# Summary scores of both query halves in 64-column halves of the array, and two groups of an expert's first step planned among the last blocks of the expert before

## The chip, the cores and the metric

The kernel runs on one NeuronCore of a Trainium2 chip. The metric is the device time of one execution in microseconds (us). Before the change four runs gave 669.8, 669.79, 671.92 and 669.19 us; their median is 669.8 us.

The core has five engines that run their own instruction streams and wait for each other through semaphores: TensorE (PE in the profile; its weight loads, which run beside the matmuls, are PEld), VectorE (DVE), ScalarE (ACT), GpSimd (POOL) and SyncE (SP). In this kernel POOL and SP mostly issue transfers.

## The reference

The first part is an attention over 4 batches, 8 heads, 768 positions and 64 numbers per head. Each query sees the keys within 15 positions of its own, and beside them 24 summaries, each standing for a block of 32 keys. The result goes into a mixture of 8 experts in which every token goes through every expert, weighted by a matrix that is normalised by rows and by columns in eight rounds.

```
k_sum = k.reshape(B, H, nb, 32, D).max(axis=3)
v_sum = v.reshape(B, H, nb, 32, D).mean(axis=3)
scores_l = scale * q @ k.T, kept where |i - j| < 16
scores_s = scale * q @ k_sum.T + log(32)
a = softmax(concat(scores_l, scores_s));  attn = a @ concat(v, v_sum)

x = attn as (3072, 512);  P = exp(x @ w_gate - max)
8 times: P /= rowsum(P); P /= colsum(P); P *= N / E
out = sum over e of P[:, e] * (relu(x @ w1[e]) @ w2[e])      # w1: 512x1024, w2: 1024x512
```

## The kernel before, in words

**Attention.** Two heads make a pair; 16 pairs, 0 to 15, four to a batch. Pairs 0 to 3 (the first batch) are worked in query halves (`pair_half`), pairs 4 to 15 whole (`pair_whole`). For a whole pair the steps on the engines are these:

- `tr` (L300) transposes keys and queries on PE for pairs 4 to 11; for pairs 12 to 15 `tr_dma` (L327) does it with a DMA that SP issues.
- `key_max` (L332, DVE) reduces the transposed keys `kT` to 24 block maxima `ks`; `key_max_split` (L338, DVE) writes them into `ksT`, columns 0 to 31 for the first head and 32 to 63 for the second, other rows zeroed. Columns 64 to 127 of `ksT` are zero.
- `scores` (L344, PE) makes the windowed scores: contraction over 64 rows, the two heads in the two row halves of the array. `score_exp` (L403, ACT) takes their exponential; `masks` (L407) and `edges` (L415, L419) on DVE cut the window out.
- `summaries` (L449, PE) multiplies all 128 columns of `ksT` with one half of the queries, 384 columns, into a PSUM bank `ss`. It is called once for each of the two query halves, each with a bank of its own. `summary_exp` (L459, ACT) reads the first 64 partitions of each.
- `near_values` (L372, L374) moves the values of neighbouring blocks into `Ve` by four small DMAs, for pairs below 12 from SP, for the others from POOL. `block_sums` (L352, PE) sums values by block.
- `values` (L430, L436, PE) makes the weighted values `av` of one half of the pair, `normalize` (L527, L528, DVE) divides, `to_xT` (L535, PE) or a DMA (L545) transposes into `xT`.

**Expert 0** needs no wait for the whole batch of tokens: when half a batch of `xT` is there (eight halves of 384 tokens), `expert0` runs its hidden layer (L208, 8 groups of 4 matmuls of 384 columns) and its projection (L213, matmuls of 512 columns), whose unscaled result is copied into `out_acc` (L204). These matmuls fill PE while the attention's vector work runs.

**Routing.** After the last batch's logits (`logits`, L555) the eight rounds of normalisation start. Each takes four DVE instructions (`sink_rows`, L564 to L568), a small matmul (`sink_cols`, L574) and two more DVE instructions (`sink_apply`, L577, L578). The last round gives `P`.

**Experts 1 to 7** use seven products for each two by two block product. Tokens are taken in three groups of 1024 for each expert (`g` counts the groups through all experts). The first step of a group consists of four `quad`s: seven products of two matmuls of 512 columns each (L742), with copies (L204), sums and relus (L764, L199) between them, and sums of the hidden blocks (`h_sum`, L776). The second step of a group consists of four `pair`s (L793), whose results are scaled by `P` and added into `out_acc`. Sums of tokens (`x_sum`, L696) and of weights (`w1_sum`, L707; `w2_sum`, L717) come before. The weights of expert 1 are loaded by POOL after the last transposed `xT` has landed.

**Order.** Nothing in the text of the kernel fixes the order on an engine. A small planner (`Plan`) holds every step as a unit with an engine, an assumed cost, its dependencies, a priority (the lower comes first) and the PSUM buffers that it opens. It simulates the engines with these costs, and where several units could start within 0.02 us of each other on an engine, it takes the one with the lowest priority number. The instructions are then issued in the planned order, and every engine runs its own list strictly in that order. So a changed cost, dependency or priority can move instructions on every engine. PSUM banks are rings in the plan: three `m` banks (expert 0, among others), three `a` banks (attention, among others), one double bank `s` for scores. The units that the change touches, and those around them:

```
U["ss", i, h] = add("PE", 0.17, lambda h=h: summaries(i, h, "a"),
                    [U["km", i], U["kT", i, 1], U.get(("A", i - NE, 1))], prio, opens=[buf])
U["sx", i, h] = add("ACT", 0.46, lambda h=h: summary_exp(i, h), [U["ss", i, h]], prio, uses=[buf])
pr = 1000.0 + n                              # expert 0's half n, 0 to 7
pr = 2000.0 + 10.0 * (HF * g + q)            # quad q of group g
```

Of the kernel before, what the change touches and what calls it, by code (L numbers as in the profile page):

```python
# [33 lines left out]
class Plan:  # L34
# [7 lines left out]
    def add(self, eng, cost, fn, deps=(), prio=0.0, opens=(), uses=(), lag=0.0):  # L42
        u = Unit(eng, cost, fn, [d for d in deps if d is not None], prio, list(opens), lag)
        for b in list(opens) + list(uses):
            b.users.append(u)
        if uses and eng != "PE":
            u.prio -= 100.0
        self.units.append(u)
        return u
# [79 lines left out]
def kernel(  # L129
# [10 lines left out]
    nc = tc.nc  # L140
# [12 lines left out]
    W = 16  # L153
    LIVE = 128 + 2 * W
    PADL = LIVE + 2 * W
    HS = S // 2
# [61 lines left out]
    NB = PB  # L218
    NE = 2
# [3 lines left out]
    with tc.manual_schedule():  # L223
# [11 lines left out]
        qT = [attn.tile([128, W + S + W], BF16, name=f"qT{i}") for i in range(NB)]  # L235
        kT = [attn.tile([128, S], BF16, name=f"kT{i}") for i in range(NB)]
# [13 lines left out]
        HF = KF // 2  # L250
# [8 lines left out]
        def bank(tag, name, dtype=FP32):  # L259
            pool, n = (mps, 3) if tag == "m" else (aps, NA)  # L260
            return pool.tile([128, 2048 // mybir.dt.size(dtype)], dtype, tag=tag, name=name, bufs=n)
# [177 lines left out]
        def summaries(i, h, tag):  # L439
            r = i % NB  # L440
            ss, rhs = bank(tag, "ss"), qT[r][:, W + h * HS:W + (h + 1) * HS]
            at["ss", i, h] = ss
            if i < PB and not h:
                for j in range(2):
                    p = slice(64 * j, 64 * j + 64)
                    nc.tensor.matmul(ss[32 * j:32 * j + 32, 0:HS], lhsT=ks[r][p, 0, :], rhs=rhs[p],
                                     start=True, stop=True)
                return
            nc.tensor.matmul(ss[:, 0:HS], lhsT=ksT[r][:], rhs=rhs, start=True, stop=True)  # L449

        def summary_exp(i, h):
            if i < PB:
# [469 lines left out]
        def pair_whole(i, prio):  # L922
            U["near", i] = add("SP" if i < BY_DMA else "POOL", 2.4 if i < BY_DMA else 3.0, lambda: near_values(i),
                               [U["v", i], U.get(("A", i - NE, 1)), U["vc", i % NE]], prio, lag=3.5)
            x1 = []
            deps = [U["kT", i, 0], U["kT", i, 1], U.get(("ed", i - 2))]
            bufs = [Buffer("s")] + (2 * [None] if i < WHOLE else [Buffer("a"), Buffer("a")])
            U["S", i, 0] = U["S", i, 1] = add("PE", 0.4 if i < WHOLE else 0.6, lambda: scores(i), deps, prio,
                                              opens=[x for x in bufs if x is not None])
            U["X", i, 0] = add("ACT", 0.97, lambda: score_exp(i, 0), [U["S", i, 0]], prio, uses=bufs[:1])  # L930
            if i < WHOLE:
                buf = Buffer("s")
                U["S", i, 1] = add("PE", 0.4, lambda: scores_1(i), deps, prio, opens=[buf])
                U["X", i, 1] = add("ACT", 0.97, lambda: score_exp(i, 1), [U["S", i, 1], U["X", i, 0]], prio,
                                   uses=[buf])
            else:
                x1 = [add("ACT", 0.53, lambda j=j: score_exp(i, 1, j), [U["S", i, 0], U["X", i, 0]], prio,
                          uses=bufs[1 + j:2 + j]) for j in range(2)]
                U["X", i, 1] = x1[1]
            for h in range(2):  # L940
                U["mk", i, h] = add("DVE", 0.56, lambda h=h: masks(i, h),
                                    [U["X", i, h], *x1[:h], U.get(("A", i - 2, 1))], prio)
            U["ed", i] = add("DVE", 0.78, lambda: edges(i),
                             [U["X", i, 0], U["X", i, 1], U["mk", i, 1], U.get(("A", i - NE, 1)), U["ec", i % NE]], prio)
            for h in range(2):
                buf = Buffer("a")
                U["ss", i, h] = add("PE", 0.17, lambda h=h: summaries(i, h, "a"),
                                    [U["km", i], U["kT", i, 1], U.get(("A", i - NE, 1))], prio, opens=[buf])
                U["sx", i, h] = add("ACT", 0.46, lambda h=h: summary_exp(i, h), [U["ss", i, h]], prio, uses=[buf])
            for h in range(2):  # L950
                buf = Buffer("a")
                U["A", i, h] = add("PE", 0.4, lambda h=h: values(i, h),
                                   [U["mk", i, h], U["ed", i], U["sx", i, h], U["Vs", i], U["near", i]],
                                   prio, opens=[buf])
                U["no", i, h] = add("DVE", 0.75, lambda h=h: normalize(i, h),
                                    [U["A", i, h], U.get(("x", i - 2))], prio, uses=[buf])
            if i >= X_BY_DMA and i % PB < PB - 1:
                U["xt", i] = add("SP", 1.5, lambda: x_dma(i), [U["no", i, 0], U["no", i, 1]], prio)
                U["x", i] = add("DMA", 1.7, None, [U["xt", i]], prio, lag=2.0)
                return  # L960
            buf = Buffer("a")
            U["xt", i] = add("PE", 0.35, lambda: to_xT(i), [U["no", i, 0], U["no", i, 1]], prio, opens=[buf])
            U["x", i] = add({"ACT": 0.8, "DVE": 0.55}, 0, lambda: x_out(U["x", i].on, i), [U["xt", i]], prio,
                            uses=[buf])
# [156 lines left out]

        def quad(e, p, q):
            g = (e - 1) * NPAIR + p
            pr = 2000.0 + 10.0 * (HF * g + q)
            buf = {t: Buffer(t) for t in "ARQ"}
            old = [U["Yp", (g - 2) // NPAIR + 1, (g - 2) % NPAIR, c, n] for c in range(4) for n in range(1, 8)] if g >= 2 else (
                [] if 2 * g + q // 2 != 3 else [U["pj", h0, c] for h0 in halves[-2:] for c in range(HG)])

            def mul(n, deps, opens=False):
                tag = {2: "R", 5: "Q", 3: "Q"}.get(n, "A")  # L1130
                u = add("PE", 0.435, lambda: product(e, p, q, n), deps, pr,
                        **{"opens" if opens else "uses": [buf[tag]]})
                U["C", e, p, q, n] = u
                return u

            def keep(n, dep):
                u = add(ANY, 0, None, [dep], pr, uses=[buf["Q" if n == 5 else "A"]])
                u.fn = lambda: snap(u.on, e, p, q, n)
                return u

            def fin(blk, deps):
                return add("DVE", 0.7, lambda: add_relu(e, p, q, blk), deps + old, pr,
                           uses=[buf[("R", "Q", None, "A")[blk]]])

            def evac(blk, dep):
                u = add("ACT", 0.6, None, [dep] + old, pr, uses=[buf["AR"[blk == 0]]])
                u.fn = lambda: evac_relu(u.on, e, p, q, blk)
                return u

            W, X = (lambda i: U["w1", e, i]), (lambda i: U["x", p, i])  # L1150
            p1 = mul(1, [U["w1", e]], True)
            sd = add(ANY, 0, None, [p1, U["bits"]], pr - 100.0, opens=[buf["R"]])
            sd.fn = lambda: seed(sd.on, e, p, q)
            buf["A"].users.append(sd)
            p2 = mul(2, [sd])
            c11 = evac(0, p2)
            p5 = mul(5, [W(0), X(0)], True)
            s5 = keep(5, p5)
            p6 = mul(6, [sd, W(1), X(1)])
            s6 = keep(6, p6)  # L1160
            p7 = mul(7, [s6, W(3), X(3)])
            c22 = fin(3, [p7, s5])
            p3 = mul(3, [s5, W(2)])
            c12 = fin(1, [p3, s6])
            p4 = mul(4, [c22, X(2)])
            c21 = evac(2, p4)
            U["H", e, p, q] = [c11, c12, c21, c22]
            if q % 2:
                h = U["H", e, p, q - 1] + U["H", e, p, q]
                d1 = add("DVE", 0.69, lambda: h_sum(e, p, q // 2, 0), h, pr - 90.0)  # L1170
                d2 = add("DVE", 0.69, lambda: h_sum(e, p, q // 2, 1), [d1], pr - 90.0)
                d3 = add("DVE", 0.69, lambda: h_sum(e, p, q // 2, 2), [d2], pr - 90.0)
                d4 = add("DVE", 0.69, lambda: h_sum(e, p, q // 2, 3), [d1], pr - 90.0)
                U["D", e, p, q // 2] = {1: h, 2: h, 4: h, 5: [d1], 6: [d2], 3: [d3], 7: [d4]}
# [120 lines left out]
```

## Time and profile before

| what | value |
|---|---|
| median of four runs | 669.8 us |
| the profiled execution, its own time | 669.8 us |
| its span, first to last instruction | 667.8 us |
| granted TensorE clock | 1.0 in nearly all of the span |
| PE busy | 658.6 us, 99% |
| DVE busy | 548.0 us, 82% |
| ACT busy | 410.2 us, 61% |
| POOL busy | 198.2 us, 30% |
| chain that ended last | PE 94%, DVE 3%, DMA 2% |
| attention and expert 0 | up to about 119 us |
| routing rounds beside the rest of expert 0 | 119 to 147 us |
| experts 1 to 7 | 150 us to the end |

The profile comes from one execution, which took 2.0 us more than its span. A matmul's row gives its start and its modelled length, which is longer than the distance to the next matmul's start, since matmuls follow each other through the array. So "busy" on PE hides short waits: what PE really loses is found from the distances between starts.

### The profile page before, as it was taken

To read this page: it belongs to the slowest core of one execution; us is meant where nothing else is said; L and a number is where in the kernel's file an instruction comes from. 1 tells how busy PE (TensorE), PEld (TensorE's weight loads), DVE (VectorE), ACT (ScalarE), POOL (GpSimd) and SP (SyncE) were. 2 spreads that over 40 slices of the span, in tenths; PEclk is the share of its full clock that TensorE was granted. 3 is DMA by queue.
4 is the path that set the end of the run, shared out by engine and by line. 5 is a ranking of instruction groups with operands and counts; after the bars stand their busy time and mean duration, and the time that the engine had idled before them with its cause. 6 is when DMAs were issued, how large, how long until landed. Compare 5 with 4: busy or idle time off the path is not lost.

```text
span 667.8 us, 13271 instructions
## 1 busy us (share of the span) xinstructions
PE 658.6 (99%) x5131; PEld 436.1 (65%) x5131; DVE 548.0 (82%) x1034; ACT 410.2 (61%) x769; POOL 198.2 (30%) x256
## 2 busy tenths in 40 slices
PE   8999999999999999999999999999999999999996
PEld 4666656654666666666666666666666666666665
DVE  7889968799879787888789887888778877988776
ACT  6667765559855656566555665656565656556652
POOL 8899713000222121222221222222122213222123
PEclk9999999999999999999999999999999999999999
DMA  9999962707333747473654756473847465334656
GB/s 167 176 146 143 130 84 43 127 1 126 56 56 65 127 67 124 75 130 65 95 98 74 125 83 106 70 126 61 123 71 128 79 95 95 64 64 111 158 134 198
DMA packets 112542, 67.89 MB, mean 102 GB/s; under 512 B 77920, under 2 KB 90464, under 8 KB 112480
## 3 DMA queue, kind: packets, MB, share of 16 engines
q0 software_dynamic: 94800, 57.46, 65.0%
q1 hardware_dynamic: 17152, 9.58, 6.1%
q8 instruction: 40, 0.66, 0.4%
q14 instruction: 22, 0.18, 0.1%
q10 hardware_dynamic: 528, 0.02, 0.0%
HBM read 52.45 MB, written 6.29 MB: 88 GB/s over the span
## 4 chain that ended last, share of the span: by engine, by line
PE 94%; DVE 3%; DMA 2%; issue 0%; ACT 0%; SPq 0%; DVEq 0%
PE yps L793 22%; PE pA L742 22%; PE pY L793 17%; PE pQ L742 11%; PE hps L208 5%; PE pR L742 5%; PE yps L213 5%; DMA kT<-kst 1%; PE sg L344 1%; PE av L497 1%; DMA kvf<-in_v_dram 1%; PE vs L352 1%; PE ss L449 1%; PE tx L535 1%; PE tkq L300 1%; PE av L436 1%
## 5 line engine op out<-in xcount | busy, mean ns | idle before, releaser
L793 PEld LDWEIGHTS <-h 128*128 128x128 f16 x2352 | 230.1, 98 | 90.2 <-issue 1.0
L821 POOL DMA_DIRECT2D out_acc<-y x120 | 101.3, 879 | 388.1 <-ACT y L817 107.3
L817 ACT ACTIVATE y<-pY,P_sb 128x256 f32<-128x256 f32 x168 | 79.9, 476 | 130.1 <-PE pY L793 128.2
L808 DVE SCALAR_TENSOR_TENSOR out_acc<-yps,P_sb,out_acc 128x512 f32<-128x512 f32 x128 | 95.1, 745 | 29.1 <-PE yps L793 29.0
L776 DVE TENSOR_TENSOR h<-h 128x1024 f16<-128x1024 f16 x168 | 109.0, 684 | 1.4
L793 PE MATMUL pY<-w,h 128*128 128x256 f16 x672 | 100.3, 273 | 0.6 <-ACT y L817 0.6
L742 PE MATMUL pA<-xT,w 128*128 128x512 f16 x336 | 98.4, 379 | 0.4 <-DVE snap L204 0.4
L793 PE MATMUL yps<-w2sum,h 128*128 128x256 f16 x672 | 98.2, 273 | 0.0
L793 PE MATMUL yps<-w,h 128*128 128x256 f16 x672 | 93.8, 273 | 0.0
L808 DVE SCALAR_TENSOR_TENSOR out_acc<-pY,P_sb,out_acc 128x512 f32<-128x512 f32 x84 | 62.9, 749 | 32.5 <-PE pY L793 31.2
L742 PEld LDWEIGHTS <-w 128*128 128x128 f16 x672 | 65.7, 98 | 32.4 <-issue 1.2
L742 PEld LDWEIGHTS <-w1sum 128*128 128x128 f16 x504 | 49.3, 98 | 45.0 <-issue 0.5
L764 DVE CUSTOM_DVE_ANT_0 h<-pQ,snap 128x512 f16<-128x512 f32 x84 | 57.6, 685 | 5.8 <-ACT snap L204 3.6
L764 DVE CUSTOM_DVE_ANT_0 h<-pA,snap 128x512 f16<-128x512 f32 x84 | 57.4, 683 | 5.7 <-PE pA L742 5.4
L199 ACT ACTIVATE h<-pA 128x512 f16<-128x512 f32 x84 | 50.7, 603 | 11.4 <-PE pA L742 11.2
L199 ACT ACTIVATE h<-pR 128x512 f16<-128x512 f32 x84 | 50.1, 596 | 7.0 <-PE pR L742 6.8
L793 PE MATMUL pY<-w2sum,h 128*128 128x256 f16 x336 | 50.4, 273 | 0.0
L204 ACT COPY pR<-pA 128x512 f32<-128x512 f32 x81 | 46.3, 571 | 6.2 <-PE pA L742 5.4
L742 PE MATMUL pA<-xsum,w 128*128 128x512 f16 x168 | 50.0, 379 | 0.0
L742 PE MATMUL pQ<-xT,w1sum 128*128 128x512 f16 x168 | 50.0, 379 | 0.0
L742 PE MATMUL pA<-xsum,w1sum 128*128 128x512 f16 x168 | 50.0, 379 | 0.0
L742 PE MATMUL pQ<-xsum,w1sum 128*128 128x512 f16 x168 | 50.0, 379 | 0.0
(145 smaller groups left out, 851.7 us busy)
## 6 DMA issues: line engine op xcount, KB each, us to landing
out_acc<-y POOLq DMA_DIRECT2D x120, 256.0 KB, 3.3
w<-in_moe_w_dram POOLq DMA_DIRECT2D x15, 1024.0 KB, 9.6
out_dram<-out_acc SPq DMA_DIRECT2D x24, 256.0 KB, 2.5
qst<-in_q_dram POOLq DMA_DIRECT2D x32, 96.0 KB, 5.6
vx<-in_v_dram POOLq DMA_DIRECT2D x15, 192.0 KB, 6.7
kst<-in_k_dram POOLq DMA_DIRECT2D x24, 96.0 KB, 6.0
w<-in_moe_w_dram POOLq DMA_DIRECT2D x4, 256.0 KB, 7.0
kst<-in_k_dram POOLq DMA_DIRECT2D x3, 192.0 KB, 4.4
```

The source lines that it names most:

```text
L199: nc.scalar.activation(out=out, in_=in_, func=AF.Relu, bias=0.0, scale=1.0)
L204: (nc.scalar.copy if eng == "ACT" else nc.vector.tensor_copy)(out=out, in_=in_)
L208: nc.tensor.matmul(hp[:, 0:n], lhsT=w1s[e][:, dk, f * 128:(f + 1) * 128], rhs=xT[:, dk, t0:t0 + n], start=(dk == 0), stop=(dk == KD - 1))
L213: nc.tensor.matmul(yp[:, d], lhsT=h[:, f, c * 128:(c + 1) * 128], rhs=w2s[e][:, f, d], start=(f == 0), stop=(f == KF - 1))
L300: nc.tensor.transpose(t[:, g * 128:(g + 1) * 128], st[:, g, :, :].rearrange("p j d -> p (j d)"), ident)
L742: nc.tensor.matmul(dst[:], lhsT=lhsT, rhs=rhs, start=first and k == 0, stop=k == HK - 1, skip_group_check=True)
L764: nc.vector._custom_dve(dve_ops.TENSOR_ADD_SAT, out=ring(e, p, q)[:, q % 2, blk, :], in0=at[src, e, p, q][:], in1=at.pop(("snap", n, e, p, ...
L776: nc.vector.tensor_tensor(out=h[:, :, out_, :], in0=h[:, :, a, :], in1=h[:, :, b, :], op=op)
L793: nc.tensor.matmul(dst[:, d], lhsT=lhsT, rhs=rhs, start=f == 0 and n in (1, 5, 2), stop=f == HF - 1, skip_group_check=True)
L808: nc.vector.scalar_tensor_tensor(out=o, in0=y, scalar=scalar, in1=o, op0=ALU.mult, op1=ALU.add)
L817: nc.scalar.activation(out=at[key][:, d], in_=src, func=AF.Copy, bias=0.0, scale=P_sb[:, t, e:e + 1])
L821: nc.gpsimd.dma_start(out=o, in_=at.pop(("y", e, p, c, key))[:], accum_op=ALU.add)
```

## The change

Two edits.

1. For the whole pairs (4 to 15) the two calls of `summaries` become one unit, `summaries_2`. It uses only the 64 columns of `ksT` that are not zero, and issues two matmuls of 384 columns: the first half of the queries goes into partitions 0 to 63 of a PSUM bank, the second half into partitions 64 to 127 of the same bank. The planner's cost is 0.22 for both instead of 0.17 for each, and one `a` bank is opened instead of two. `summary_exp` reads its 64 partitions as before.
2. The priority of the quads of groups 0 and 1 (expert 1's first 2048 tokens) is no longer 2000 and more, but between 1006 and 1007.75, and so among those of expert 0's last two halves (1006 and 1007).

```
+        def summaries_2(i):
+            r, ss = i % NB, bank("a", "ss")
+            for h in range(2):
+                at["ss", i, h] = ss[64 * h:64 * h + 64]
+                nc.tensor.matmul(ss[64 * h:64 * h + 64, 0:HS], lhsT=ksT[r][:, 0:64],
+                                 rhs=qT[r][:, W + h * HS:W + (h + 1) * HS], start=True, stop=True)
...
+            buf = Buffer("a")
+            U["ss", i, 0] = U["ss", i, 1] = add("PE", 0.22, lambda: summaries_2(i),
+                                                [U["km", i], U["kT", i, 1], U.get(("A", i - NE, 1))], prio, opens=[buf])
             for h in range(2):
-                buf = Buffer("a")
-                U["ss", i, h] = add("PE", 0.17, lambda h=h: summaries(i, h, "a"),
-                                    [U["km", i], U["kT", i, 1], U.get(("A", i - NE, 1))], prio, opens=[buf])
                 U["sx", i, h] = add("ACT", 0.46, lambda h=h: summary_exp(i, h), [U["ss", i, h]], prio, uses=[buf])
...
         def quad(e, p, q):
             g = (e - 1) * NPAIR + p
-            pr = 2000.0 + 10.0 * (HF * g + q)
+            pr = 2000.0 + 10.0 * (HF * g + q) if g > 1 else 1006.0 + 0.25 * (HF * g + q)
```

## The prediction

> **What bounds the kernel now.** I read the engine lines of the page first, then the groups by line, then PE's timeline by starts, the chain, and DVE's share by windows.
>
> ```profile
> PE 658.6 (99%) x5131; PEld 436.1 (65%) x5131; DVE 548.0 (82%) x1034; ACT 410.2 (61%) x769; POOL 198.2 (30%) x256
> ...
> L449 PE MATMUL ss<-qT,ksT 128*128 128x384 bf16 x28 | 8.6, 329 | 0.0
> ...
> L446 PE MATMUL ss<-qT,ks 64*32 64x384 bf16 x8 | 1.3, 332 | 0.0
> ```
>
> PE sets the time. Taking for each shape the distance between starts where matmuls follow each other (0.216 us for 512 columns, 0.109 for 256, 0.162 for 384), all PE distances that are longer than that add up to 17 us of the span; from 180 to 640 us they add up to nothing. So only work removed from PE, or a wait removed before 180 us, can pay. The two other lines hold a hint: 28 summary matmuls over the full array busy PE 8.6 us, but 8 of the first batch, which sit in different quarters of the array two by two, busy it 1.3 us, half of 8 x 332 ns: they overlap.
>
> ```profile
> 8.60 0.53 PE L297 MATMUL tkq<-ident,kst 128*64 128x128 bf16 x12
> 9.05 0.38 PE L309 MATMUL tkq<-ident,qst 64*64 64x64 bf16 x12
> 9.36 0.34 PE L446 MATMUL ss<-qT,ks 64*32 64x384 bf16 x2
> ...
> 60.70 0.34 PE L436 MATMUL av<-Ve,Ee 128*128 128x130 bf16 x3
> 60.88 0.34 PE L430 MATMUL av<-vx,em 128*128 128x65 bf16 x6
> 61.05 0.34 PE L436 MATMUL av<-Ve,Ee 128*128 128x130 bf16 x3
> 61.32 0.38 PE L344 MATMUL sg<-qT,kT 64*128 64x160 bf16 x6
> ...
> 63.60 0.51 PE L300 MATMUL tkq<-ident,kst 128*128 128x128 bf16 x6
> 63.94 0.33 PE L449 MATMUL ss<-qT,ksT 128*128 128x384 bf16 x1
> ```
>
> Columns of the timeline: start, length of the group, line, shape of the array (rows*columns) and data. Three `Ve` matmuls take 0.18 us when the same array shape follows (60.70 to 60.88) and 0.27 when the shape changes (61.05 to 61.32): a change of shape costs PE 0.09. Twelve transposes in 64-column halves take 0.45 with the change behind them (8.60 to 9.05), six full ones 0.34 (63.60 to 63.94): the halves run side by side, and the change costs 0.11.
>
> ```profile
> 86.17 0.95 DVE L332 TENSOR_REDUCE ks<-kT 128x24 bf16<-128x768 bf16 x1 [2.67 <-DMA kT<-kst]
> ...
> 86.73 0.51 PE L352 MATMUL vs<-vx,m_blk 128*128 128x128 bf16 x6
> 88.04 0.81 PE L208 MATMUL hps<-xT,w 128*128 128x384 f16 x4 [0.81 <-DVE out_acc L204]
> 88.69 0.35 PE L430 MATMUL av<-vx,em 128*128 128x65 bf16 x6
> 89.13 0.52 PE L436 MATMUL av<-Ve,Ee 128*128 128x130 bf16 x3
> 89.67 0.34 PE L430 MATMUL av<-vx,em 128*128 128x65 bf16 x6
> ...
> 153.17 0.59 PE L742 MATMUL pQ<-xT,w1sum 128*128 128x512 f16 x2
> 154.12 0.59 PE L742 MATMUL pA<-xT,w 128*128 128x512 f16 x2 [0.35 <-DVE snap L204]
> ...
> 155.41 0.59 PE L742 MATMUL pA<-xsum,w1sum 128*128 128x512 f16 x2
> 155.95 0.59 PE L742 MATMUL pA<-xsum,w 128*128 128x512 f16 x2
> 156.55 0.59 PE L742 MATMUL pQ<-xT,w1sum 128*128 128x512 f16 x2
> ```
>
> Two places of waiting. At 86 us DVE stands 2.67 us for pair 13's `kT` (DMA transpose, issued at 77.08, landed after 9.1); the copy out of `yps`, a mask and edges queue behind it. PE loses 1.31-0.34 = 0.97, then 0.44-0.18 = 0.26 and 0.54-0.18 = 0.36: **1.6 us**. At expert 1's start a pair of product matmuls takes 0.43, but 0.95, 0.54 and 0.60 at 153 to 156: 0.80, and three later ones to 166 us add 0.2: **1.0 us**.
>
> **Part 1, column halves.** It removes 24 matmuls of 0.162 and adds 12 couples of 0.162 each plus under 0.01 for the second start (L446: two in 0.34, one is 0.33). Saved: 12 x 0.16 = 1.9. But the couples have another array shape than their neighbours. In the order in which the built programs issue, PE's array shape changes 93 times before and 113 times after. The 20 added changes cost 0.09 to 0.11 each: 1.8 to 2.2, I take 1.9. Sum of part 1: **0.0**, bounds -0.1 and +0.3. If the halves ran one after the other, +1.9. Their weight loads (0.11 us, L297) are hidden as those of L297 are, twelve of which do not keep matmuls from starting 0.028 apart on the mean.
>
> [...]
>
> **What part 1 moves.** The shorter unit and the freed `a` bank change the plan from 37 us on. On DVE, the reduction of pair 13's `kT` (L332) now stands behind pair 11's masks, edges and a relu, and behind it stands only pair 11's normalisation. On SP its transpose now stands ahead of the four `Ve` transfers of pair 11, not behind them. So it starts earlier and is needed later, and the 1.6 us go. What is late next: those four transfers wait for the end of pair 9's `values`. In the new order PE has 9.7 us of matmuls between that end and pair 11's first use of `Ve` (13.9 before). Needed: 0.6 to the first issue (73.73 to 74.32), 2.0 to the last (74.32 to 76.32), then the landing, for SP's `Ve` transfers 4.5 at 61 us, 5.3 at 69, 8.4 at 74. Sum 7.1 to 11.0: between hidden and 1.3 late. POOL issues its last attention load at 75.8; the transfers now fall after 79, so I take a value near the short end and put 0.2 down. The five transposes behind them come up to 2.4 later; their score matmuls follow 8 us or more after the landing, and behind pair 14's reduction on DVE nothing stands that PE needs within 4 us. POOL's order is the same.
>
> **Part 2, the earlier quads.** Nothing is added or removed; products of groups 0 and 1 move between the rounds and expert 0's rest. Between the first and the eighth routing matmul PE now has 64 matmuls of 384 columns (10.4), 60 of 512 (13.0), 74 of products (16.0) and 7 routing steps of 0.14 (1.0): 40.4 us where it had 23.9. DVE has in the same stretch 7 rounds of 2.17 (0.63 from 122.57 to the row sums, 1.54 from there) and 34 other instructions at about 0.63: 15.2 + 21.4 = 36.6. The first product comes 15.5 us of PE work after pair 14's `values`; its weights landed 12.6 after them (111.67 to 116.31, and 8.0). ACT's copies and relus move along, over windows in which ACT is 49 to 86% busy. POOL's load of expert 2's second weights waits for expert 0's last projection, about 12 us later now, and expert 1's accumulating transfers queue behind it; the first of these ran at 174.36, by sums that load is issued near 165. So products no longer stand behind fresh copies and sums: the 1.0 us go. New waits where quads and pairs are mixed otherwise: below nothing is excluded, since no wait other than the 1.0 is there to lose; above, as much as now, 1.0; I take 0.1, after the rows from 180 us on, which have none.
>
> **Sum.** 669.8 is the profiled execution's own time (span 667.8 and 2.0 around it), and the median. 669.8 + 0.0 - 1.6 + 0.2 - 1.0 + 0.1 = **667.5**, span 665.5.
>
> **Rivals.** (1) Late `Ve` and new waits at their upper ends: 667.5 + 1.1 + 0.9 = 669.5 at most, 668.6 in the middle. For it: DMA is nearly full until 86 us. (2) The change does not do what it says: the two halves read different queries from the same 128 partitions, while L297's couples read the same identity. If they are served in turn: 667.5 + 1.9 = 669.4. Against it: L446, but there the partitions differ too. (3) Slower: the routing chain on DVE. PE executes in order and stands at each routing matmul until DVE has made its column sums; DVE now must also wait there for products, copies and ACT.
>
> ```profile
> 140.00:160.00 20.00, 19.64 (x102) 9.74 (x101) 18.31 (x37) 16.14 (x30) 1.64 (x2) 1.00 0.42 65
> ...
> 180.00:200.00 20.00, 20.00 (x139) 13.33 (x138) 14.72 (x22) 12.34 (x25) 4.63 (x6) 1.00 0.38 66
> ```
>
> The fourth number is DVE's busy time. PE gives it 40.4 and 1.4 before the first round (4.07 of PE work after the last logits, 2.65 needed), 41.8 for 36.6: 12% idle is free. At 140 to 160 us it idles 8%, at 180 to 200 26%. At 26% it needs 49.7, and PE stands 7.9: 675.4; at 17%, half way, 44.1 and 2.3: 669.8. It decides from 12% on; its middle is 672.5. (4) The array changes cost less beside 384-column matmuls, or further short waits go: 666.
>
> **How the numbers follow.** Forecast 0.56, rival (1) 0.16, (2) 0.08, (3) 0.14, (4) 0.06. Under 0.3%, 2.0 us, a measurement of this kernel can hardly tell a change from none. The forecast is 2.3 below, so close to that line that I count 0.08 of its 0.56 as within it: faster 0.48 + 0.06 = 0.54, within 0.16 + 0.08 + 0.08 = 0.32, slower 0.14. The range: at the low end part 1's bound, no late `Ve` and a part of (4), 666.4; at the high end (1) and (2) whole, and of (3) its milder part, 670.0.
>
> **What would show it.** Right: `ss` couples whose two rows last 0.34 together; matmuls after a couple starting 0.10 late; no gap at pair 13's reduction; no long distances between products up to 180 us; routing matmuls without PE waits. Wrong: an `ss` couple lasting 0.49, PE waiting for `Ve` of pair 11, or for DVE before routing matmuls 5 to 8.

## The result, and the profile after

The changed kernel takes 668.4 us in the median of 44 runs, the kernel before 670.8 in the median of 70. The ratio is 0.9971 with a 95% interval of 0.9961 to 0.9981: 1.9 us less (1.3 to 2.6; the two medians alone lie 2.4 apart), where 2.3 was forecast. That is right on the 0.3% below which the prediction counts a change as none. The absolute forecast, 667.5, is 0.9 low, because its base of 669.8 (four runs) lay 1.0 below the median of the seventy.

The profiled execution of the changed kernel took 669.3 us with a span of 667.6, only 0.2 less than before. Two lines of it are the engine line of the page and the group of the new summaries (line, engine, array shape, count, busy us, mean ns of one).

```profile
PE 657.5 (99%) x5131; PEld 434.5 (65%) x5131; DVE 547.0 (82%) x1030; ACT 414.7 (62%) x773; POOL 198.2 (30%) x256
...
L455 PE MATMUL ss<-qT,ksT 128*64 128x384 bf16 x24 | 4.2, 350 | 0.0
```

24 matmuls of 0.350 that keep PE busy for 4.2 us, half of 24 x 0.350: the two halves of a couple run side by side, as the forecast said. PE's timeline by starts shows what stands around one couple, and why this span hides the gain:

```profile
41.38 0.36 PE L430 MATMUL av<-vx,em 128*128 128x65 bf16 x6
43.46 0.40 PE L436 MATMUL av<-Ve,Ee 128*128 128x130 bf16 x3 [1.72 <-DMA Ve<-vx]
...
43.88 0.34 PE L436 MATMUL av<-Ve,Ee 128*128 128x130 bf16 x3
44.14 0.35 PE L455 MATMUL ss<-qT,ksT 128*64 128x384 bf16 x2
44.43 1.04 PE L213 MATMUL yps<-w,h 128*128 128x512 f16 x4
```

PE stands 1.9 us (by start distances) for pair 4's four `Ve` transfers, the first whole pair's. The forecast had no such wait. The couple lasts 0.35, but 0.29 pass until the next matmul starts, 0.12 more than a 384-column matmul needs (0.162), and 0.26 pass for the three matmuls ahead of it, 0.09 more than usual (0.18 in the rows at 60.70 and 60.88 of the prediction).

The places that were to get faster did. SP, PE and DVE from the transpose of pair 13's keys to their reduction (SPq is SP's queue, issuing):

```profile
77.65 1.91 SPq L327 DMA_TRANSPOSE kT<-kst  x1
80.68 0.59 SPq L372 DMA_DIRECT2D Ve<-vx  x1
...
87.49 0.50 PE L352 MATMUL vs<-vx,m_blk 128*128 128x128 bf16 x6
87.83 0.81 PE L208 MATMUL hps<-xT,w 128*128 128x384 f16 x4
...
90.30 0.34 PE L436 MATMUL av<-Ve,Ee 128*128 128x130 bf16 x3
90.42 0.94 DVE L332 TENSOR_REDUCE ks<-kT 128x24 bf16<-128x768 bf16 x1
```

The transpose is now issued ahead of pair 11's `Ve` transfers (the second row is their first). It landed at 86.26, and the reduction starts at 90.42 without a wait. The block sums (87.49 to 87.83, 0.34) are followed at once. The row at 90.30 is the first use of pair 11's `Ve`, without a wait. In the stretch of the routing, the timeline has no PE wait, and the table by windows gives the load (window, length, then busy us of PE, PEld, DVE, ACT and POOL, granted clock, DMA share, GB/s):

```profile
126.80:167.10 40.30, 40.30 (x214) 20.90 (x213) 36.78 (x79) 23.65 (x45) 1.27 (x2) 1.00 0.19 32
...
166.66 0.59 PE L749 MATMUL pA<-xsum,w 128*128 128x512 f16 x2
167.09 0.28 PE L581 MATMUL sink<-csum_sb,col_en 128*128 128x8 f32 x2
```

The products run at their pitch (two in 0.43) straight into the eighth routing matmul. DVE is busy 36.8 of 40.3 us.

**How the runs are compared below.** Two things differ from execution to execution of one and the same program: the start of expert 0's first projection (the first `yps` row of L213, between 33.2 and 36.6 us) and pair 4's wait for `Ve`. The larger delays of the first projection come from slow matmuls at the beginning. In the second profile of the whole change the six block sums at 7.8 us take 0.85 us instead of 0.50, twelve transposes at 9.57 us 0.85 instead of 0.53 (the windows show a granted clock of 1.00 there all the same), and at 11.47 us PE is already the 1.3 us late that it is at the projection. In the run with one more column sum the granted clock is 0.61 on the mean from 7 to 9 us and 0.50 from 9 to 15 us, and the projection comes at 36.6. The smaller delays, up to 0.9, stand beside waits of 0.2 to 0.3 us for loads of keys and weights. So for each profiled run the table takes both off the span; "wait" is the start distance between the last L430 matmul and the first L436 of pair 4, less its usual 0.03.

| kernel | span | first projection | wait, pair 4 | rest | median of all runs, ratio to before [95%] |
|---|---|---|---|---|---|
| before | 667.8 | 33.26 | 0.14 | 634.4 | 670.8 |
| before, second profile | 668.9 | 33.57 | 1.12 | 634.2 | 670.9 (one run) |
| whole change | 667.6 | 33.42 | 1.88 | 632.3 | 668.4, 0.9971 [0.9961, 0.9981] |
| whole change, second profile | 666.7 | 34.56 | 0 | 632.1 | 668.4, 0.9978 [0.9959, 0.9996] |
| halves only | 667.9 | 33.28 | 0 | 634.6 | 670.8, 1.0014 [0.9993, 1.0035] |
| quads only | 666.9 | 33.25 | 0.45 | 633.2 | 670.2, 0.9992 [0.9977, 1.0007] |
| order of the change, full array | 665.1 | 33.27 | 0 | 631.8 | 668.9, 0.9979 [0.9959, 0.9999] |

The rest is 2.1 us shorter after the change, and it repeats within 0.2.

### The profile page after: what moved, and what is told of

Same layout as the page of the kernel before. It is cut to its first block, busy times and chain, and to the rows that moved or that the text cites. A ratio compares the mean times of both kernels' runs of the same rounds, so it can differ in the third digit from the quotient of the medians.

```text
span 667.6 us, 13244 instructions
## 1 busy us (share of the span) xinstructions
PE 657.5 (99%) x5131; PEld 434.5 (65%) x5131; DVE 547.0 (82%) x1030; ACT 414.7 (62%) x773; POOL 198.2 (30%) x256
## 4 chain that ended last, share of the span: by engine, by line
PE 93%; DMA 3%; POOL 2%; issue 0%; SPq 0%; DVE 0%; ACT 0%; POOLq 0%; DVEq 0%
PE yps L800 22%; PE pA L749 22%; PE pY L800 17%; PE pQ L749 11%; PE yps L213 6%; PE hps L208 6%; PE pR L749 5%; DMA w<-in_moe_w_dram 1%; DMA vx<-in_v_dram 1%; DMA Ve<-vx 1%; PE sg L344 1%; PE av L430 1%; PE av L436 1%; PE tkq L300 1%; PE vs L352 1%; PE tx L542 0%
## 5 line engine op out<-in xcount | busy, mean ns | idle before, releaser
L199 ACT ACTIVATE h<-pR 128x512 f16<-128x512 f32 x84 | 50.1, 596 | 8.6 <-PE pR L749 8.1
```

What stands on the lines that cost most here:

```text
L199: nc.scalar.activation(out=out, in_=in_, func=AF.Relu, bias=0.0, scale=1.0)
```

## The experiments

**The parts, and the whole once more.** Halves only: the line of `quad` as it was before.

```diff
-pr = 2000.0 + 10.0 * (HF * g + q) if g > 1 else 1006.0 + 0.25 * (HF * g + q)
+pr = 2000.0 + 10.0 * (HF * g + q)
```

> The column halves alone; the quads of expert 1 keep their old place. My theory, from the trace after the change: the wait of 1.6 us at pair 13's key reduction goes here too, because the planned order up to expert 1 is the one of the whole change; the couples themselves bring nothing (12 x (0.325 - 0.285) us saved, 7 or 8 entries of 0.093 us added: +0.2). So 1.4 us less than before, and the 1.0 us of waits between products at 153 to 166 us stands as it was. Rival: the gain comes from the quads alone, and what pair 13 gave is lost again at pair 4's wait for Ve (1.9 us at 41.5 us in the trace after): then 0 to +0.5 us against before. On that wait of pair 4: if it belongs to the new order, it stands here with 1.7 us or more; if it is a matter of when loads land in one execution, it differs by more than 0.5 us between the runs of this call.

Measured: a rest of 634.6, 0.2 to 0.4 longer than before, and a ratio that shows no gain. The wait behind pair 13's reduction is gone, as my theory had it. But the waits at expert 1's start, all counted, grew from 1.0 to 2.4 us, which neither theory had. Four of them make 2.05; the three longest:

```profile
152.29 0.59 PE L749 MATMUL pQ<-xT,w1sum 128*128 128x512 f16 x2 [0.35 <-DVE snap L204]
154.85 0.59 PE L749 MATMUL pA<-xT,w 128*128 128x512 f16 x2 [0.17 <-ACT snap L204]
161.41 0.59 PE L749 MATMUL pA<-xsum,w 128*128 128x512 f16 x2 [0.79 <-DVE h L771]
```

So 1.3 to 1.6 gained at pair 13, 1.4 lost here and 0.35 lost by the array shape (below) add up to 0.2 to 0.5 longer, close to the measured 0.2 to 0.4.

Quads only: the kernel before with the new line of `quad` alone.

> The earlier quads alone; summaries in full-array matmuls as before. My theory: the waits between products behind fresh copies and sums go, 1.0 us less than before; the wait of 1.6 us for pair 13's kT at 86 us stands as in the trace before, and PE's array shape changes stay at the old number. Rival, the routing chain on DVE: PE waits before routing matmuls and the time is equal to before or longer. Pair 4's wait for Ve: if it belongs to the new order of the halves, none here; if it is a matter of landing times, it may be here as well.

Measured: rest 633.2, 1.0 to 1.2 less than before. No PE wait is left between products up to 180 us or at routing matmuls; the wait at 87 us stands (start distances 0.7 longer than usual behind the block sums, 0.6 in the rows after). The ratio is the weaker measure of it: from 1.5 us less to 0.5 more.

The whole change again:

> The whole change once more, for its place beside the parts on the same chip and for a second profile. My theory: 1.9 us less than before (ratio 0.997), the sum of the two parts run alone, 1.4 + 1.0 less a few tenths. Pair 4's wait for Ve at 41.5 us (1.9 us in the first profile): by landing times, another length in this profile, and a span near 665.6 us where it is missing; by the new order, 1.7 us or more again and a span of 667.6 us.

Measured: no wait at pair 4, but the first projection came 1.1 to 1.3 later than in the runs beside it, so the span is 666.7 and not 665.6. The two parts do not add: +0.3 and -1.1 alone, -2.1 together.

**The array shape alone.** Same order of instructions, `ksT` widened to 192 columns with zeros on both sides, both matmuls into one bank over the full array:

```diff
-nc.tensor.matmul(ss[64 * h:64 * h + 64, 0:HS], lhsT=ksT[r][:, 0:64],
-                 rhs=..., start=True, stop=True)
+nc.tensor.matmul(ss[:, 0:HS], lhsT=ksT[r][:, 64 - 64 * h:192 - 64 * h],
+                 rhs=..., start=not h, stop=bool(h))
```

> The whole change with its planned order, but each summary matmul takes the full array again: the weights are padded with 64 zero columns before or behind, and the two matmuls accumulate into one bank, so that partitions 0 to 63 and 64 to 127 hold the same as with the halves. Only the array shape differs from the whole change. My theory, from the trace after: a couple takes 0.285 us with its exit and 0.093 us for the entry from a full-array matmul, two full matmuls take 0.325: 0.2 to 0.3 us faster than the whole change. By the terms of the prediction (0.162 for a couple, 20 changes of 0.09 to 0.11): 0.0, from -0.3 to +0.1. Rival, the halves bring what their doubled rate promises (the changes of shape cost nothing that counts): 1.9 us slower than the whole change. Pair 4's wait for Ve as for the other runs of this call.

The same place in both timelines, the whole change (second profile) first, then the full array:

```profile
43.07 0.34 PE L436 MATMUL av<-Ve,Ee 128*128 128x130 bf16 x3
43.33 0.35 PE L455 MATMUL ss<-qT,ksT 128*64 128x384 bf16 x2
43.62 1.04 PE L213 MATMUL yps<-w,h 128*128 128x512 f16 x4
```

```profile
41.82 0.34 PE L436 MATMUL av<-Ve,Ee 128*128 128x130 bf16 x3
41.99 0.49 PE L455 MATMUL ss<-qT,ksT 128*128 128x384 bf16 x2
42.31 1.03 PE L213 MATMUL yps<-w,h 128*128 128x512 f16 x4
```

From the `Ve` matmuls to the projection 0.55 with halves, 0.49 with the full array. Over all twelve couples, by start distances: the second matmul starts after 0.003 instead of 0.162 to 0.173 (1.95 saved); the matmul behind starts after 0.283 instead of 0.162 and itself takes 0.011 longer (12 x 0.131 = 1.57 lost); eight couples stand behind a full-array matmul and are entered 0.092 late (0.74 lost); four stand behind scores, where the shape changes either way. Sum: the halves cost **0.35 us**, a little more than the 0.2 to 0.3 of the theory from the trace. Each of the four couples behind scores gained 0.04, each of the eight others lost 0.06. The times can't tell the two apart (0.9978 and 0.9979).

**Why the halves alone brought nothing.** The halves-only kernel, with less DVE work ahead of expert 1 (the lines in brackets are in words):

```diff
 def sink_rows():
-    (row sums, reciprocal, multiplication in every round)
+    (row sums, reciprocal, multiplication in the first round only)
```

> The column halves alone (quads in their old place), and seven of the eight routing rounds leave out the row sums, their reciprocals and the multiplication by them (0.35 + 0.30 + 0.36 us on DVE, 7.1 us in all; the routing weights are then others). Question: why did the halves alone bring nothing? My theory: PE came to expert 1's start 2 us earlier, but DVE did not, so the waits between products grew there from 1.0 to 2.1 us. With 7.1 us less on DVE ahead of that place they go: excess of PE's start distances between 148 and 170 us under 0.3 us (2.1 with the halves alone). Rival: the waits belong to the order of products, copies and sums in the plan, whatever DVE's load is: they stay at 1 us or more.

Measured: DVE busy 16.1 us of 25.0 in the routing where it had been 22.1 of 24.4, and the same waits, 2.05 us in the same four; the longest:

```profile
163.11 0.59 PE L749 MATMUL pA<-xsum,w 128*128 128x512 f16 x2 [0.79 <-DVE h L771]
```

My theory falls: DVE's load in the routing is not the cause. What is left is the order that the planner wrote, which no run varied by itself; DVE's timeline shows three sums of `h` (2.0 us) issued just ahead of the combination that this product waits for, in both runs. Moving the quads replaces that order, and these waits are gone in the whole change, so the gain at pair 13 survives only with both parts.

**How much DVE had free.** One and three more column sums in each of the eight rounds (0.50 us each):

```diff
-            nc.vector.tensor_reduce(out=csum_sb[:], ...)
+            for _ in range(2): nc.vector.tensor_reduce(out=csum_sb[:], ...)   # 4 in the second kernel
```

> The whole change with the column sums of each routing round made twice on DVE (0.50 us each, 3.5 us more between the first and the eighth routing matmul); nothing else differs. By the sum of the prediction DVE has 36.6 us of work for 41.8 us there, so 5.2 us are free: no new PE wait, span as that of the whole change (665.4 to 667.6). By the trace after, DVE is busy 38.9 of 40.3 us between these matmuls: 1.4 us free, so PE waits 2.1 us or more between 133 and 170 us. By the rival with the routing chain, PE already stands at routing matmuls, and all 3.5 us are added.

> As the run with one more column sum in each round, with three more (10.5 us more on DVE between the first and the eighth routing matmul). By the sum of the prediction 10.5 - 5.2 = 5.3 us of PE waits; by the trace after 10.5 - 1.4 = 9.1 us; by the rival 10.5 us. The difference to the run with one more is 7.0 us by the last two, 5.3 by the first.

Measured between the last logits and expert 1's first projection: 45.62 us in the whole change, 46.89 with one more, 55.42 with three more. So 4.0 us of added work cost 1.27 and 12.0 cost 9.80: 2.7 and 2.2 us were free, between the 5.2 of the prediction and the 1.4 that I read from the trace. That 1.4 came from adding up durations (38.9) which overlap at their ends; the table by windows, with 36.8 busy, leaves 3.5. The waits of the run with three more name who is late, and no longer only at the routing matmuls (engine, line, releaser: us in total, times, longest):

```profile
PE pA L749 <- DVE h L771: 2.8, 3, 1.2
PE sink L581 <- DVE csum_sb L575: 2.7, 2, 1.6
```

**Pair 4's wait for `Ve`.** First remedy: its values load issued on POOL ahead of the edge constants (and no longer behind them), once with the halves and once with the full array.

```diff
 load("w2", lambda: load_w2(0), 0.85, 5.0)
+load_pair(PB, "v")
 for n in range(NE):
     U["vc", n] = ...
```

> The whole change, and pair 4's values load issued on POOL ahead of the constants of the edge buffers instead of behind them, 4 us earlier; nothing else moves on any engine. Question: is pair 4's wait for its Ve transfers (1.9 us at 41.5 us in the first profile of the change, 0.4 with the quads alone, none in the other three profiles) the slack that the landing of that load leaves? If so: SP issues the four transfers 2 us earlier or more (34 to 35 us before), no wait at that place in the profile, a span of 665.4 to 665.8 us, and a median 0.5 to 1.0 us below that of the whole change, with the same fastest executions (667.2). Rival: the spread of the times comes from elsewhere (the loads of the first 12 us): the median stays within 0.3 us of the whole change.

> The order of the whole change, full-array summaries padded with zeros as in the run before (no column halves), and pair 4's values load 4 us earlier. Candidate for a version faster than both. By the ledger of array shapes 0.3 us below the same with column halves, span 665.1 us, fastest executions at 666.8, ratio to before 0.996 to 0.997. If the halves are worth their doubled rate, it is 1.9 us slower than the same with halves instead.

It failed. With the halves the load went out 4 us earlier (24.4 instead of 28.4) and landed 11.2 us later instead of 6.6: it gained nothing, and PE waited 2.8 us. It landed 1.5 and 1.6 us after the 1 MB of `w2` that was issued ahead of it in these two runs, and 1.7 us after it in the whole change, so it seems to stand behind that load wherever it is issued. The median, 669.2 (0.9983 [0.9969, 0.9998]), is no better than the whole change; with the full array it was 668.3 (0.9977 [0.9962, 0.9993]), with a rest of 631.8 and, in that execution, no wait. After the long wait the granted clock was lower too (windows of the run with the halves, columns as above; the third number from the end is the granted clock):

```profile
44.00:45.00 1.00, 0.00 (x0) 0.00 (x0) 0.00 (x0) 0.00 (x0) 1.00 (x3) 1.00 2.60 137
...
47.00:48.00 1.00, 1.00 (x8) 0.27 (x6) 0.36 (x1) 0.14 (x1) 1.00 (x2) 0.50 2.35 152
48.00:49.00 1.00, 1.00 (x12) 0.95 (x11) 0.89 (x3) 0.84 (x1) 1.00 (x2) 0.50 2.10 138
```

Second remedy: let the planner put pair 4's values later, by telling it the landing time that the traces show.

```diff
 U["near", i] = add("SP" ..., [U["v", i], ...],
-                   prio, lag=3.5)
+                   prio, lag=6.0 if i == PB else 3.5)   # 7.0 in the second kernel
```

> The order of the whole change with full-array summaries, and the planner told that pair 4's Ve transfers land 6.0 us after their issue (3.5 in all others), which is what the traces show for the last of them (6.0 to 7.2). Pair 4's values then stand about 2.6 us of PE work later, and the order after them is planned anew. If the Ve wait is the spread's cause: no PE wait at pair 4 in the profile, a span of 665.0 to 665.3 us, the median within 0.7 us of the lowest time (667.5 or less). If the new order brings other waits: they show between 45 and 120 us, and the time is that of the whole change or above.

> As the run with 6.0 us, with 7.0: pair 4's values stand about 4 us of PE work later than in the whole change. Same expectations; the wait at pair 4 is then excluded for every landing seen so far (up to 7.2 us after the issue), and if the median is not below that of the run with 6.0, the spread of the times comes from elsewhere.

Pair 4's wait is gone in both, and both new orders brought other ones: rests of 635.1 and 633.1, ratios 0.9991 [0.9979, 1.0002] and 0.9973 [0.9961, 0.9985]. With 7.0 the nine executions lie between 668.0 and 669.3 us, where the 44 of the whole change go from 667.2 to 673.5, so the wait may well be a part of that spread. But nine are few, and another part is missing among them: all nine executions of the whole change with a mean granted clock of 0.990 or less took 672.0 us or more, and none with 7.0 is below 0.997. With 6.0, pair 11's values came to stand where its `Ve` had not landed:

```profile
85.97 0.35 PE L430 MATMUL av<-vx,em 128*128 128x65 bf16 x6
88.40 0.40 PE L436 MATMUL av<-Ve,Ee 128*128 128x130 bf16 x3 [2.08 <-DMA Ve<-vx]
```

**The kernel before, once more.**

> The kernel before, unchanged but for blank lines that bring its line numbers to those of the kernel after, for a second profile of it. Three readings rest on its one profile so far. From the first projection of expert 0 to the end, less pair 4's wait for Ve, it took 634.4 us (632.2 after the change, 631.8 with full-array summaries in the same order): expected here 634.3 to 634.6. PE's wait behind pair 13's key reduction: 1.6 us, 1.3 to 1.6 with the quads alone; expected again over 1 us. Pair 4's wait for its Ve transfers, 0.1 us: if it is a matter of when loads land, anything from 0 to 2.8 us; if only the new order can make it long, under 0.5.

Measured: a rest of 634.2, 0.1 under what I expected; behind the block sums at 88 us a start distance 0.7 longer than usual, 1.3 with the rows after; and pair 4 waits 1.1 us for `Ve` in the old order too. That wait is a matter of landing times: in the ten profiles of kernels in which nothing that leads to it differs, it was 0 in four and 0.1 to 2.2 us in six, of both orders. No version is shown to be faster than the whole change by its times; the full array in the same order is 0.35 us shorter by the trace.

## Why the prediction was right, point by point

**What bounds the kernel.** Right: all of the change's effect is in PE's start distances before 180 us.

**Part 1, the array.** The mechanism was right and the size of one term was off. Saved 1.95 (1.9 forecast) and 20 added changes of shape, as counted; but they cost 2.3 and not 1.9, 0.116 each: 0.092 on entry as the `Ve` rows had it, 0.131 on the way out of a couple, above the 0.11 taken from the transposes. The sum is +0.35, just outside the bounds of -0.1 and +0.3. The runs show the delays at the borders, not what the array does in them. That two halves run in the time of one is seen in the 0.003, and is lost again at the borders.

**Part 1, the plan.** The 1.6 us at pair 13 went in every kernel with the new order and stood (1.3 to 1.6) in every one with the old, and by the mechanism forecast: counted from the first projection and less pair 4's wait, the transpose was issued 1.3 us earlier (42.35 instead of 43.68 us) and DVE came to the reduction 5 us later (55.1 instead of 50.1). Both were needed in the first profile: the keys landed at 51.0 by this count, so at the old place DVE would still have waited 0.9. Pair 11's late `Ve`, put down with 0.2, did not come: issued at 80.7 to 82.7 ("after 79"), landed in at most 6.6 us, by 88.8, and first used at 90.3, 1.5 to spare. That the mechanism is real, the kernel with a lag of 6.0 shows, with 2.1 us.

**Part 2.** The 1.0 us went, by itself (1.0 to 1.2) and in the whole, and the 0.1 for new waits did not come. What the prediction did not see is that the parts depend on each other: without part 2, part 1's order at expert 1's start costs the 1.4 us more that makes it worthless. It summed two parts that were only ever to run together, and was saved by that.

**The sum.** Luck helped: the array cost 0.35 more than forecast, and the 0.3 put down for late `Ve` and new waits did not come. The two misses nearly cancel, so the trace's 2.1 us lie closer to the forecast 2.3 than its terms do.

**The rivals.** (2), halves in turn, is refuted by the 0.003. (3), the routing chain on DVE, was nearer than its 0.14 looked: the load was forecast well (36.6 of 41.8; measured 36.8 of 40.3), but not what is free, 2.2 to 2.7 us instead of 5.2. The idle shares that it took for what DVE needs, 17 and 26%, were too high: DVE idles 9% here and PE does not wait, and with three more column sums, where PE does wait, DVE idles 5% (47.3 us busy of 49.7 between the first and the eighth routing matmul).

**What it left out.** Pair 4's wait for `Ve`, up to 2.8 us, which differs between the profiles of both kernels and all but hides the gain in the first one of each (667.8 and 667.6). By the sum the span was to be 665.5; the first profile less that wait is 665.7.

## What to carry to other kernels

Before narrowing matmuls to run them side by side, count the borders: here a couple saved 0.16 us and each change of array shape cost 0.09 to 0.13, so a lone couple between full-array matmuls lost 0.06, and one that stood where the shape changes anyway gained 0.04. By these numbers it should pay where several couples stand together, which no run tried. When an order is planned from costs, edits do not add: run the parts alone and together, and compare the stretch behind the loads, not spans, when landing times differ from run to run. An early issue is no early landing: here a load that was issued 4 us sooner behind a large one (at 24.4 us instead of 28.4) landed no sooner (35.6 instead of 35.0).

## What the runs showed of the hardware that was not expected

In two runs a short wait of PE was followed by half the clock. After the 1.9 us without work at pair 4 in the first profile of the change the granted clock stayed at 1.00 (40 to 48 us); after waits of 2.2 us (three more column sums) and 2.8 us (the early load) at the same place it was 0.50 for 3.4 us, in the second case from 1.3 us after work had resumed, and these runs took 1.5 to 1.6 us more than the wait itself (91.6 us from the first projection to the last logits in the one, where 88.0 and the wait make 90.2; a rest of 633.8 instead of 632.2 in the other). The length alone does not decide: the wait of 2.2 us in the run with a lag of 6.0, before the `Ve` row at 88.40, left the clock at 1.00: the rows from 88.64 on are 0.18 apart, as usual, and the mean clock of that execution is 0.999, of the two with half the clock 0.997 (windows of the run with a lag of 6.0):

```profile
86.00:87.00 1.00, 0.32 (x7) 0.20 (x5) 1.00 (x2) 0.69 (x2) 0.00 (x0) 1.00 1.79 104
87.00:88.00 1.00, 0.00 (x0) 0.00 (x0) 0.04 (x1) 0.00 (x0) 0.00 (x0) 1.00 0.88 161
```

Shorter idle times went both ways too. 1.6 us before the routing matmul at 133.90 in the run with three more column sums left the clock at 1.00 (128.6 to 178.4 us). In the run with one more, PE was busy for 0.70 of the 2.00 us from 5 to 7 us, and the clock was 0.61 on the mean of the next 2 us; in the profile before it was busy for 1.23 of them, and the clock stayed at 1.00. No run changed the length or the place of one wait alone, so what decides is not shown.

Leaving the 64-column shape cost more than entering it from the full array, in the twelve couples of the whole change: the next matmul started 0.120 late instead of 0.092, and it took 0.011 longer besides.
